# Attention probabilities turned by DMA instead of TensorE, and a band matrix with its columns in another order

## The chip, the cores and the metric

The kernel runs on one core of a Trainium2 chip. A core has TensorE (PE; its weight loads are shown as PEld), VectorE (DVE), ScalarE (ACT), GpSimd (POOL) and SyncE (SP), which here issues every DMA. The metric is the device time of one execution in microseconds (us).

## The reference

Two residual blocks over x of shape 1 x 2048 x 448, in bf16. Block A is a local attention: 16 heads of 28 channels, each position s looks at eight earlier positions s, s-2, ..., s-14. Block B mixes shifted channel groups and then runs a wide feed-forward layer (448 to 1792 to 448).

```
h  = x + A(layernorm(x)),   h2 = h + B(layernorm(h))
A: qkv = x @ wqkv; idx = pos - 2*w for w in 0..7
   logits = einsum("bhsd,bhswd->bhsw", q, k[idx]) * scale   (masked where idx < 0)
   o = einsum("bhsw,bhswd->bhsd", softmax(logits), v[idx]);  return o @ wo
B: h = gelu(layernorm(x) @ w1); hs = shift(h) @ w2; x1 = x + hs
   return x1 + gelu(layernorm(x1) @ w3) @ w4
```

## The kernel before, in words

The 2048 positions are four **blocks** of 512, each block four tiles of 128. Block A runs in phases for each block t: N1 (layer norm), A1 (turn the normalised rows, q and k), V (v), A2 (logits, softmax), A3 (probabilities times v, then wo), B1 (second layer norm, turn, w1, gelu). Block B then runs over five units of 2 or 4 tiles: B2 (w2 and the third layer norm), W3 (w3, gelu) and B3 (w4, store).

The order of the work is written out by hand. Each call of a helper makes one operation with a running number; the list `ORDER` (line 19) is a permutation of these numbers, and `arrange` (line 191) hands every operation to its engine in that order. An engine runs its own operations strictly in that order and waits by semaphore for what an operation needs from others. `OTHER` (line 50) names operations that run on their second engine. Counting the operations in the order in which the code adds them tells what each number in `ORDER` is. In `arrange` a DMA transpose waits for all plain DMAs issued since the transpose before it and for that transpose itself, and a plain DMA waits for the transpose before it. Nearly all instructions are emitted from one line of `emit_engine`, so the profile shows nearly all of them as L983 and they are told apart by tile names: `ps` is PSUM, `bd_r` the band matrix, `pb` the probabilities, `lntm` the normalised rows, `actT` turned activations, `qk_r` the products of queries and keys, and `arena` holds q, k, the turned probabilities `pt`, weights and more.

The parts that the change touches:

- **Turning the normalised rows for q, k and v** (`transposed`, line 568). With "t" TensorE turns a block in 4 steps of 8 transposes (64 partitions each) into two PSUM banks, and two copies bring them to `actT` as 128 x 1024 bf16. With "d" SP issues one DMA transpose. `TURN['A1']` is "ttdd": blocks 0 and 1 by TensorE, 2 and 3 by DMA.
- **Keys shared between groups of 64 positions** (end of `phase_A1`). The key tiles `kr` and `kk` need the last 16 positions of the group before. Four small DMAs a block (`kra`, `krb`, `krc`, `kkp`; the last block has two) copy them from SBUF to SBUF.
- **Turning the probabilities p** (end of `phase_A2`). p lies as 128 rows (head and place) by 8 groups of 80 columns in `pb`. Sixteen matmuls against the identity turn it into two PSUM banks, and two copies of 80 x 512 write `pt` with the row index n outside and the group r inside.
- **The band** (`phase_A3`). For each of four tiles VectorE multiplies `pt`, repeated 8 times, by the 80 x 64 mask `bmask`, repeated 32 times, into an 80 x 2048 bf16 tile of `bd_r` (four buffers). Its columns are ordered (n, g, r), so that the 64 columns of one head n lie side by side. TensorE then runs 32 matmuls a tile: the weights are an 80 x 32 slice of v, the moving operand the 64 columns of one head. Four of them (j = 0 to 3) write to four different groups of 32 PSUM partitions and run at the same time.

Of the kernel before, what the change touches and what calls it, by code (L numbers as in the profile page):

```python
# [6 lines left out]
ALU = mybir.AluOpType  # L7
AX = mybir.AxisListType
BF16 = mybir.dt.bfloat16
# [3 lines left out]
TURN = {'A1': 'ttdd', 'B1': 'dddd', 'B2': 'ddddd'}  # L13
NORM = {'N0': 'vvvv', 'N1': 'avvv', 'B1': 'avvv', 'B2': 'avvvv'}
STATS = {'N1': 'vvva', 'B1': 'avaa', 'B2': 'avvvv'}
NQK, NBD, NLN, NACT, NSM, NO = 3, 4, 2, 4, 1, 6
# [32 lines left out]
"""  # L49
OTHER = """  # L50
102 186 187 381 490 493 496 499 502 505 549
# [229 lines left out]
def bass_sequential_preLN__sliding_local_dilated__mixer_s_mlp__prompt_kernel(  # L281
# [9 lines left out]
    PADK = 16  # L291
# [19 lines left out]
    with ExitStack() as es:  # L311
        def sb(name, shape, dt):
            return es.enter_context(nc.sbuf_tensor(name, shape, dt))
# [6 lines left out]
        bmask = sb("bmask", [KW, 64], BF16)  # L320
        lntm = sb("lntm", [128, NLN, 4, 512], BF16)
# [20 lines left out]
        pb = sb("pb", [128, NSM, NW * KW], BF16)  # L342
# [12 lines left out]
        def arv(off, parts, n):  # L355
            return AR[0:parts, off:off + n]
# [9 lines left out]
        pt = [arv(A_KV + t * KVB + 4 * KVW, KW, 1024) for t in range(NST)]  # L366
# [39 lines left out]
        def dma(chan, out_ap, in_ap, nbytes, eng="sp", **kw):  # L406
            return S.add(eng, "dma_start", chan=chan, nbytes=nbytes, out=out_ap, in_=in_ap, **kw)
# [208 lines left out]
        def setup_late(after):  # L616

            def late(meth, **kw):
                pool(meth, after=after, **kw)

            for lo in (0, 1):
                late("tensor_copy", out=wr_s[:, :, 64 * lo:64 * lo + 64], in_=wqkv_s[:, :, 384 + D * lo:448 + D * lo])
            late("memset", ap=zc[:], constant=0.0)
            for e in range(2):
                late("tensor_copy", out=zc[:, 0:3, e, 16 * e:16 * e + 16], in_=indj[:, 0:3, :])
            late("tensor_copy", out=zc[:, 3, 0, :].rearrange("p (e h) -> p e h", e=2), in_=indj[:, 3:5, :])
            late("memset", ap=onesrow, constant=0.0)
            late("memset", ap=onesrow[0:1, 0:16], constant=1.0)
            late("memset", ap=maskrow, constant=0.0)
            for w in range(1, NW):  # L630
                lo = DIL * (NW - 1 - w)
                late("memset", ap=maskrow[:, 0:64 * w].rearrange("p (r n) -> p r n", n=64)[:, :, lo:lo + DIL], constant=-30000.0)
            late("memset", ap=kk[0][:, :, 0:PADK], constant=0.0)
            late("memset", ap=kr[0][0:64, 0, 0:PADK], constant=0.0)
            late("memset", ap=vw[0:PADK, 0, 0, :], constant=0.0)
            late("memset", ap=gT[:, :, 0:2], constant=0.0)
            late("memset", ap=gT[:, :, 2 + SEQ:4 + SEQ], constant=0.0)
# [30 lines left out]
        def phase_A1(t):  # L668
# [26 lines left out]

            duo(half(X, 0, True), half(Y, 64, False), ((0, 256),))
# [3 lines left out]
            dma("kra%d" % t, kr[t][64:128, :, 0:PADK], kr[t][0:64, :, 64:KW], 64 * 4 * PADK * 2)  # L700
            dma("krb%d" % t, kr[t][0:64, 1:4, 0:PADK], kr[t][64:128, 0:3, 64:KW], 64 * 3 * PADK * 2)
            if t + 1 < NST:
                dma("krc%d" % t, kr[t + 1][0:64, 0, 0:PADK], kr[t][64:128, 3, 64:KW], 64 * PADK * 2)
                dma("kkp%d" % t, kk[t + 1][:, :, 0:PADK], kk[t][:, :, 512:KVW], 128 * 3 * PADK * 2)
# [24 lines left out]
        def phase_A2(t):  # L729
# [34 lines left out]
            mult = dict(out=row(pb, sl * NW * KW + DIL, KW + DIL), in0=row(ls, sl * 512, 64),  # L764
                        in1=bass.AP(zs, sl * 64, [[64 * NSM, 128], [8, NW], [2, 4], [0, NW], [1, DIL]]), op=ALU.mult)
            S.add("dve", "tensor_tensor", alts=[("pool", [("tensor_tensor", mult)])], **mult)
            banks = [_Tile(P_bank), _Tile(P_bank)]

            def turn(h, r):
                part = (TOP, BOT)[h]  # L770
                return (h, dict(out=banks[h](lambda v: v[0:KW, 64 * r:64 * r + 64]), lhsT=pb[part, sl, r * KW:(r + 1) * KW], rhs=ident[part, part],
                                start=True, stop=True), 64)

            steps([turn(h, r) for r in range(NW) for h in range(2)])
            for h, b in enumerate(banks):
                copy(pt[t].rearrange("p (n r) -> p n r", r=NW)[:, 64 * h:64 * h + 64, :], b(lambda v: v[0:KW, :].rearrange("p (r n) -> p n r", r=NW)))

        def phase_A3(t):
            a = _Tile(P_act)
            sl = t % 2  # L780
            for il in range(4):
                bd = _Tile(P_bd)
                b = _Tile(P_bank)
                dve("tensor_tensor", block=True, out=bd(lambda v: v.rearrange("p (n g r) -> p n g r", g=8, r=NW)),
                    in0=pt[t][:, il * 256:il * 256 + 256].rearrange("p (n r) -> p n r", r=NW).unsqueeze(2).broadcast_to([KW, 32, 8, NW]),
                    in1=bmask[:].rearrange("p (g r) -> p g r", r=NW).unsqueeze(1).broadcast_to([KW, 32, 8, NW]), op=ALU.mult)
                mms([(b(lambda v, j=j, lo=128 * c + 64 * a2: v[32 * j:32 * j + 32, lo:lo + 64]),
                      vw[:, sl, 2 * il + a2, (4 * c + j) * 32:(4 * c + j) * 32 + 32],
                      bd(lambda v, lo=(16 * a2 + 4 * c + j) * 64: v[:, lo:lo + 64]), True, True, 64, j)
# [235 lines left out]
```

## Time and profile before

| | |
|---|---|
| median of three runs | 189.47 us (189.41 to 189.87) |
| the profiled execution | 189.32 us |
| its span, first to last instruction | 187.5 us |
| TensorE clock granted | 0.999 |

The profile is of one execution. A busy time is the union of an engine's instructions; idle time is put down to what ended it. The chain of work follows the last instruction back through what released each step. A view by windows gives the busy time of each engine in a stretch.

### The profile page before, as it was taken

Reading aid. Unit: us, or ns where it says so; the run is one execution under the profiler, and the core shown is the slowest. Engines: PE = TensorE matmul, PEld = TensorE weight load, DVE = VectorE, ACT = ScalarE, POOL = GpSimd, SP = SyncE. Lnnn points to the kernel's source line nnn. Section 1 sums busy time; section 2 is a strip of 40 time slices with the busy share of each in tenths; the row PEclk is TensorE's granted clock in tenths of the full one; section 3 lists DMA queues with packets and bytes.
Section 4 is the critical chain, followed back from the end, with each engine's and each line's share of the span. In section 5 each row is a group of like instructions: output and inputs, shape, how many; then the busy total and the mean of one; then the engine's idle time right before and its main releaser. Section 6 shows DMA issues by size and latency. Waiting matters only on the chain.

```text
span 187.5 us, 5641 instructions
## 1 busy us (share of the span) xinstructions
PE 179.2 (96%) x2434; PEld 102.4 (55%) x2434; DVE 126.6 (68%) x224; ACT 123.9 (66%) x282; POOL 29.2 (16%) x63
## 2 busy tenths in 40 slices
PE   6999999999988799999999999999999999999994
PEld 2694434355443345477445555555556665666882
DVE  7799999999999999997297278470057357000503
ACT  4679999989999897988976447505775004822340
POOL 4230000000004101004801200200002662500000
PEclk9999999999999999999999999999999999999999
DMA  5995724676644655453645000371000432400111
GB/s 133 359 286 100 105 59 101 112 177 128 144 129 75 155 144 139 121 154 104 117 126 98 3 0 3 68 149 36 0 0 3 89 96 77 105 3 0 66 36 49
DMA packets 36577, 18.06 MB, mean 96 GB/s; under 512 B 25304, under 2 KB 36040, under 8 KB 36552
## 3 DMA queue, kind: packets, MB, share of 16 engines
q1 hardware_dynamic: 36552, 17.70, 40.2%
q8 instruction: 19, 0.31, 0.7%
q14 instruction: 6, 0.05, 0.1%
HBM read 7.91 MB, written 1.84 MB: 52 GB/s over the span
## 4 chain that ended last, share of the span: by engine, by line
PE 78%; ACT 12%; DVE 4%; DMA 4%; issue 1%; SPq 0%
PE ps L983 78%; ACT arena L983 5%; ACT lntm L983 3%; DMA actT<-lntm 2%; ACT vt L983 2%; DVE st L983 1%; DMA xin<-in_A_x_dram 1%; ACT xin L983 1%; DVE lntm L983 1%; DVE bd_r L983 1%; DVE qk_r L983 1%; ACT rs_x L983 0%; DVE ls L983 0%; DVE mx L983 0%; DVE mv L983 0%
## 5 line engine op out<-in xcount | busy, mean ns | idle before, releaser
L983 PE MATMUL ps<-actT,arena 64*128 64x512 bf16 (+1 forms) x756 | 69.1, 329 | 0.4 <-ACT vt L983 0.4
L983 ACT ACTIVATE h3T<-ps 128x512 bf16<-128x512 f32 (+1 forms) x70 | 31.1, 515 | 40.8 <-PE ps L983 40.5
L983 PEld LDWEIGHTS ps<-actT,arena 64*128 64x128 bf16 x756 | 38.8, 94 | 24.9 <-PE ps L983 0.8
L983 PE MATMUL ps<-arena,h3T 64*128 64x448 bf16 (+2 forms) x434 | 43.7, 343 | 0.1
L983 ACT ACTIVATE arena<-ps 128x512 bf16<-128x512 f32 (+3 forms) x62 | 31.3, 544 | 7.0 <-PE ps L983 6.4
L983 PEld LDWEIGHTS ps<-arena,h3T 64*128 64x128 bf16 (+1 forms) x434 | 26.3, 94 | 16.1 <-PE ps L983 0.5
L983 DVE TENSOR_TENSOR qk_r<-arena 128x4096 bf16<-128x4096 bf16 (+1 forms) x16 | 32.0, 2014 | 0.0
L983 DVE SCALAR_TENSOR_TENSOR qk_r<-ps,mrs,arena 128x448 bf16<-128x448 f32 (+1 forms) x17 | 10.5, 652 | 30.9 <-PE ps L983 25.4
L983 POOL TENSOR_TENSOR arena<-arena,xin 128x448 f32<-128x448 f32 x16 | 16.1, 1037 | 19.8 <-DVE lntm L983 19.8
L983 DVE TENSOR_TENSOR bd_r<-arena,bmask 80x2048 bf16<-80x2048 bf16 x16 | 18.8, 1210 | 0.0
L983 DVE SCALAR_TENSOR_TENSOR arena<-xin,rs_y,ps 128x448 f32<-128x448 bf16 x16 | 10.2, 674 | 11.6 <-PE ps L983 9.6
L983 PE MATMUL ps<-wo_s,actT 64*128 64x448 bf16 x128 | 14.4, 350 | 1.0 <-ACT actT L983 0.7
L983 PE MATMUL ps<-w_s,arena 64*128 64x448 bf16 (+1 forms) x128 | 14.2, 350 | 0.4 <-ACT arena L983 0.3
L983 PE MATMUL ps<-actT,w_s 64*112 64x512 bf16 x112 | 13.4, 379 | 0.8 <-DMA actT<-lntm 0.6
L983 PE MATMUL ps<-arena,actT 64*128 64x448 bf16 x112 | 12.4, 350 | 0.1
L983 ACT ACTIVATE lntm<-xin,nm 128x448 bf16<-128x448 bf16 x16 | 10.5, 663 | 2.4 <-DVE nm L983 2.4
L983 POOL TENSOR_TENSOR pb<-ls,mx 128x512 bf16<-128x512 f32 x2 | 3.5, 1730 | 48.3 <-ACT mx L983 48.3
L983 ACT ACTIVATE actT<-ps 128x512 bf16<-128x512 f32 (+2 forms) x18 | 10.6, 645 | 0.0
L983 PEld LDWEIGHTS ps<-actT,w_s 64*112 64x112 bf16 x112 | 7.1, 127 | 6.3 <-PE ps L983 1.0
L983 PEld LDWEIGHTS ps<-wo_s,actT 64*128 64x128 bf16 x128 | 5.8, 94 | 7.6 <-ACT actT L983 1.9
L983 PEld LDWEIGHTS ps<-w_s,arena 64*128 64x128 bf16 (+1 forms) x128 | 6.4, 94 | 6.6 <-PE ps L983 1.0
L983 DVE BATCH_NORM_STATS2 st<-xin 128x6 f32<-128x448 bf16 x16 | 9.1, 614 | 0.9 <-DMA xin<-in_A_x_dram 0.9
(71 smaller groups left out, 160.9 us busy)
## 6 DMA issues: line engine op xcount, KB each, us to landing
arena<-in_B_w_dram SPq DMA_DIRECT2D x2, 896.0 KB, 5.5
out_dram<-qk_r SPq DMA_DIRECT2D x15, 112.0 KB, 1.8
arena<-in_B_w_dram SPq DMA_DIRECT2D x2, 784.0 KB, 5.0
vw<-vt SPq DMA_DIRECT2D x4, 320.0 KB, 3.2
vw<-vt SPq DMA_DIRECT2D x4, 256.0 KB, 4.7
arena<-in_A_wqkv_dram SPq DMA_DIRECT2D x2, 448.0 KB, 4.5
xin<-in_A_x_dram SPq DMA_DIRECT2D x2, 448.0 KB, 6.9
xin<-in_A_x_dram SPq DMA_DIRECT2D x3, 224.0 KB, 5.2
```

What stands on the lines that cost most here:

```text
L983: inst = getattr(eng, meth)(**kw)
```

## The change

1. `TURN['A1']` becomes "tttt": the normalised rows of blocks 2 and 3 are turned by TensorE.
2. The four key DMAs become copies out of PSUM (helper `last`), on ScalarE, 14 in all.
3. p is turned by one DMA transpose a block; `pb` is padded to 128 columns a group, and `pt` has r outside and n inside. The 16 matmuls and the two copies are gone.
4. The band has its columns ordered (g, r, n). The mask is spread once over an 80 x 2048 tile `band` by GpSimd, so that all three operands of the multiplication have runs of 32 in n. The moving operand of head n is now every 32nd column. `bd_r` has three buffers in place of four.
5. `ORDER` and `OTHER` are new. By the numbers, p of block 2 stays on GpSimd and p of block 3 goes to VectorE; SP issues the turns "B1 of block 0, p of block 2, B1 of block 1" one after another with no plain DMA between them; the second pair of v matmul steps of block 3 moves to just ahead of the w1 matmuls of block 0.

```
-TURN = {'A1': 'ttdd', ...}
+TURN = {'A1': 'tttt', ...}
-NQK, NBD, NLN, NACT, NSM, NO = 3, 4, 2, 4, 1, 6
+NQK, NBD, NLN, NACT, NSM, NO = 3, 3, 2, 4, 1, 6
...
+        band = sb("band", [KW, 2048], BF16)
...
+            late("tensor_copy", out=band[:].rearrange("p (m n) -> p m n", n=32), in_=bmask[:].unsqueeze(2).broadcast_to([KW, 64, 32]))
...
+            def last(b, lo, n):
+                return b(lambda v: v[64:128, 0:256].rearrange("p (j n) -> p j n", j=4)[:, lo:lo + n, 64 - PADK:])
...
-            dma("kra%d" % t, kr[t][64:128, :, 0:PADK], kr[t][0:64, :, 64:KW], 64 * 4 * PADK * 2)
-            dma("krb%d" % t, kr[t][0:64, 1:4, 0:PADK], kr[t][64:128, 0:3, 64:KW], 64 * 3 * PADK * 2)
+            copy(kr[t][64:128, :, 0:PADK], last(X, 0, 4), False)
+            copy(kr[t][0:64, 1:4, 0:PADK], last(Y, 0, 3), False)
             if t + 1 < NST:
-                dma("krc%d" % t, kr[t + 1][0:64, 0, 0:PADK], kr[t][64:128, 3, 64:KW], 64 * PADK * 2)
-                dma("kkp%d" % t, kk[t + 1][:, :, 0:PADK], kk[t][:, :, 512:KVW], 128 * 3 * PADK * 2)
+                copy(kr[t + 1][0:64, 0:1, 0:PADK], last(Y, 3, 1), False)
+                copy(kk[t + 1][:, :, 0:PADK], kk[t][:, :, 512:KVW])
...
-            banks = [_Tile(P_bank), _Tile(P_bank)]
-            def turn(h, r):
...
-            steps([turn(h, r) for r in range(NW) for h in range(2)])
-            for h, b in enumerate(banks):
-                copy(pt[t].rearrange("p (n r) -> p n r", r=NW)[:, 64 * h:64 * h + 64, :], ...)
+            dma_turn("turnp", pt[t].rearrange("p (r n) -> p r n", r=NW), pb[:, sl, :])
...
-                dve("tensor_tensor", block=True, out=bd(lambda v: v.rearrange("p (n g r) -> p n g r", g=8, r=NW)),
-                    in0=pt[t][:, il * 256:il * 256 + 256].rearrange("p (n r) -> p n r", r=NW).unsqueeze(2).broadcast_to([KW, 32, 8, NW]),
-                    in1=bmask[:].rearrange("p (g r) -> p g r", r=NW).unsqueeze(1).broadcast_to([KW, 32, 8, NW]), op=ALU.mult)
+                dve("tensor_tensor", block=True, out=bd(lambda v: v.rearrange("p (g r n) -> p g r n", g=8, r=NW)),
+                    in0=pt[t][0:KW, :].rearrange("p (r n) -> p r n", r=NW)[:, :, 32 * il:32 * il + 32].unsqueeze(1).broadcast_to([KW, 8, NW, 32]),
+                    in1=band[:].rearrange("p (g r n) -> p g r n", g=8, r=NW), op=ALU.mult)
...
-                      bd(lambda v, lo=(16 * a2 + 4 * c + j) * 64: v[:, lo:lo + 64]), True, True, 64, j)
+                      bd(lambda v, n=16 * a2 + 4 * c + j: v[:, n::32]), True, True, 64, j)
```

More of the change, by code (lines that the diff above doesn't have):

```diff
@@ L12 @@
 _LAST = {}
-TURN = {'A1': 'ttdd', 'B1': 'dddd', 'B2': 'ddddd'}
+TURN = {'A1': 'tttt', 'B1': 'dddd', 'B2': 'ddddd'}
 NORM = {'N0': 'vvvv', 'N1': 'avvv', 'B1': 'avvv', 'B2': 'avvvv'}
 STATS = {'N1': 'vvva', 'B1': 'avaa', 'B2': 'avvvv'}
-NQK, NBD, NLN, NACT, NSM, NO = 3, 4, 2, 4, 1, 6
+NQK, NBD, NLN, NACT, NSM, NO = 3, 3, 2, 4, 1, 6
 POWER = {'N1': 'aaaa', 'B1': 'aaaa', 'B2': 'apapp'}
@@ L19 @@
 ORDER = """
[29 rows of a table removed]
[29 rows of a table added]
 """
 OTHER = """
-102 186 187 381 490 493 496 499 502 505 549
+91 103 186 187 383 460 465 499
 """
@@ L341, in bass_sequential_preLN__sliding_local_dilated__mixer_s_mlp__prompt_kernel @@
         indj = ls[:, NSM - 1, 0:40].bitcast(BF16).rearrange("p (c h) -> p c h", c=5)
-        pb = sb("pb", [128, NSM, NW * KW], BF16)
+        pb = sb("pb", [128, NSM, NW * 128], BF16)
         ost = qk_r[:, 0, 0:NO * D].rearrange("p (k n) -> p k n", n=D)
@@ L365, in bass_sequential_preLN__sliding_local_dilated__mixer_s_mlp__prompt_kernel @@
         kr = [arv(A_KV + t * KVB + 3 * KVW, 128, 4 * KW).rearrange("p (j n) -> p j n", j=4) for t in range(NST)]
-        pt = [arv(A_KV + t * KVB + 4 * KVW, KW, 1024) for t in range(NST)]
+        pt = [arv(A_KV + t * KVB + 4 * KVW, 128, 1024) for t in range(NST)]
         maskrow = arv(A_KV + (NST - 1) * KVB, 1, 512)
@@ L763, in phase_A2 @@
             row = lambda v, off, step: bass.AP(v, off, [[v.shape[1] * v.shape[2], 128], [step, NW], [16, 4], [DIL, NW], [1, DIL]])
-            mult = dict(out=row(pb, sl * NW * KW + DIL, KW + DIL), in0=row(ls, sl * 512, 64),
+            mult = dict(out=row(pb, sl * NW * 128 + DIL, 128 + DIL), in0=row(ls, sl * 512, 64),
                         in1=bass.AP(zs, sl * 64, [[64 * NSM, 128], [8, NW], [2, 4], [0, NW], [1, DIL]]), op=ALU.mult)
             S.add("dve", "tensor_tensor", alts=[("pool", [("tensor_tensor", mult)])], **mult)
-            banks = [_Tile(P_bank), _Tile(P_bank)]
-            def turn(h, r):
-                part = (TOP, BOT)[h]
-                return (h, dict(out=banks[h](lambda v: v[0:KW, 64 * r:64 * r + 64]), lhsT=pb[part, sl, r * KW:(r + 1) * KW], rhs=ident[part, part],
-                                start=True, stop=True), 64)
-            steps([turn(h, r) for r in range(NW) for h in range(2)])
-            for h, b in enumerate(banks):
-                copy(pt[t].rearrange("p (n r) -> p n r", r=NW)[:, 64 * h:64 * h + 64, :], b(lambda v: v[0:KW, :].rearrange("p (r n) -> p n r", r=NW)))
+            dma_turn("turnp", pt[t].rearrange("p (r n) -> p r n", r=NW), pb[:, sl, :])
         def phase_A3(t):
```

58 rows, old and new, of the table ORDER are left out of this document.

## The prediction

> **What bounds the kernel now.** I read the busy shares first, then the chain, then the windows on both sides of the first w3 matmul (81.3 us).
>
> ```profile
> PE 179.2 (96%) x2434; PEld 102.4 (55%) x2434; DVE 126.6 (68%) x224; ACT 123.9 (66%) x282; POOL 29.2 (16%) x63
> PE 78%; ACT 12%; DVE 4%; DMA 4%; issue 1%; SPq 0%
> 34.00:81.30 47.30, 43.72 (x824) 21.16 (x823) 46.51 (x62) 43.73 (x99) 3.48 (x4) 1.00 0.56 130
> 81.30:184.30 103.00, 102.94 (x1234) 63.48 (x1231) 47.43 (x104) 52.15 (x114) 20.45 (x23) 1.00 0.25 60
> ```
>
> The reader is to see two kernels in one. From 81.3 us to 184.3 us TensorE never rests (102.94 of 103.00), so a matmul more or less there is time more or less. From 34.0 to 81.3 us three engines are nearly full at once: VectorE 46.51 of 47.30, TensorE 43.72, ScalarE 43.73. All that better scheduling can win in this stretch is the 3.6 us in which TensorE idles. Its largest waits lie around the w1 matmuls of block 0:
>
> ```profile
> 58.57 0.93 PE L983 MATMUL ps<-wo_s,actT 64*128 64x448 bf16 x8 [0.74 <-ACT actT L983]
> 61.47 0.49 PE L983 MATMUL ps<-ident,pb 64*80 64x64 bf16 x16 [0.59 <-POOL arena L983]
> 62.60 3.77 PE L983 MATMUL ps<-actT,w_s 64*112 64x512 bf16 x28 [0.65 <-DMA actT<-lntm]
> 66.30 0.99 PE L983 MATMUL ps<-bd_r,vw 80*32 80x64 bf16 x96
> 67.56 0.93 PE L983 MATMUL ps<-w_s,arena 64*128 64x448 bf16 x8 [0.26 <-ACT arena L983]
> ```
>
> (Start, length, what, and in brackets the idle time before it with its releaser.) The 28 w1 matmuls wait for the DMA transpose of block 0's second layer norm; the only work between was the turn of p.
>
> **The change part by part.** *Turns on TensorE.* The turn of p is 16 matmuls; the turn of a block of normalised rows is 8 + 24 transposes.
>
> ```profile
> 48.06 0.46 PE L983 MATMUL ps<-ident,pb 64*80 64x64 bf16 x16
> 48.36 0.81 PE L983 MATMUL ps<-actT,arena 64*128 64x512 bf16 x6
> 12.73 0.30 PE L983 MATMUL ps<-ident,lntm 64*128 64x64 bf16 x8
> 12.97 0.83 PE L983 MATMUL ps<-actT,arena 64*128 64x256 bf16 x12
> 13.63 0.51 PE L983 MATMUL ps<-ident,lntm 64*128 64x64 bf16 x24
> 13.98 2.81 PE L983 MATMUL ps<-arena,actT 64*128 64x448 bf16 x28
> ```
>
> What counts is start to next start, since the ends overlap: 0.30 us for a p turn, 0.24 + 0.35 = 0.59 us for a block. Four p turns go (-1.2 us), two blocks come (+1.2 us): **zero**.
>
> *The band's moving operand.* This is the step that decides. The 64 columns of a head now lie 64 bytes apart. The volume is 4 blocks x 4 tiles x 8 = 128 groups of four concurrent matmuls.
>
> ```profile
> 100.99 1.29 PE L983 MATMUL ps<-bd_r,vw 80*32 80x64 bf16 x128
> 72.12 1.05 PE L983 MATMUL ps<-qk_r,zc 128*32 128x512 bf16 x16
> L983 PE MATMUL ps<-qk_r,zc 128*32 128x512 bf16 x112 | 7.5, 382 | 0.0
> L983 PE MATMUL ps<-bd_r,vw 80*32 80x64 bf16 x512 | 5.9, 195 | 0.4 <-DVE bd_r L983 0.3
> ```
>
> Now, 128 matmuls (32 groups) last 1.29 us, less the last one's own 0.195: 34 ns a group. The logits matmuls show what a column costs in the same mode: (1.05 - 0.38) / 3 = 0.22 us for 512 columns, 0.44 ns a column, 28 ns for 64. They read runs of 16 adjacent elements; no row shows TensorE reading elements apart. Bounds: **zero** if it reads them as fast, and four streams one after another, 4 x 28 - 34 = 78 ns more a group, **+10.0 us**. Below nothing there is no reason for a gain, the matmuls being the same. Between, the rows of VectorE are the nearest:
>
> ```profile
> L983 DVE TENSOR_TENSOR qk_r<-arena 128x4096 bf16<-128x4096 bf16 x12 | 27.3, 2281 | 0.0
> L983 DVE TENSOR_TENSOR qk_r<-arena 128x2048 bf16<-128x2048 bf16 x4 | 4.9, 1214 | 0.0
> L983 DVE SCALAR_TENSOR_TENSOR qk_r<-ps,mrs,arena 128x448 bf16<-128x448 f32 x15 | 9.6, 679 | 25.0 <-PE ps L983 19.4 <-POOL arena L983 4.9 <-DMA out_dram<-qk_r 0.5
> L983 DVE SCALAR_TENSOR_TENSOR qk_r<-ps,mrs,arena 128x224 bf16<-128x224 f32 x2 | 0.9, 451 | 5.9 <-PE ps L983 5.9
> L983 DVE TENSOR_TENSOR bd_r<-arena,bmask 80x2048 bf16<-80x2048 bf16 x16 | 18.8, 1210 | 0.0
> ```
>
> Adjacent bf16 take VectorE (2281 - 1214) / 2048 = 0.52 ns each, single 4-byte elements (679 - 451) / 224 = 1.02 ns: two neighbours for the price of one access. TensorE's 0.44 ns a column is again about half of such an access. I take it that its rate rests on pairs too, and that elements apart go at half rate: 28 ns more a group, less the 6 ns of slack now in 34, so 2.8 to 3.6 us, and I take **+3.2 us**. The multiplication itself stays at 1210 ns, since it has pairs before and after.
>
> [...]
>
> *ScalarE.* Gone: eight copies of p (seven on ScalarE). Added: four copies of turned rows, 14 small copies.
>
> ```profile
> L983 ACT ACTIVATE arena<-ps 80x512 bf16<-80x512 f32 x7 | 3.9, 591 | 0.0
> L983 ACT ACTIVATE actT<-ps 128x1024 bf16<-128x1024 bf16 x2 | 2.0, 1061 | 0.0
> L983 ACT ACTIVATE mx<-mx 128x64 f32<-128x64 f32 x8 | 2.1, 263 | 0.1
> L983 ACT ACTIVATE rs_y<-rs_x 128x4 f32<-128x4 f32 x12 | 2.5, 208 | 0.2
> L983 ACT ACTIVATE arena<-ps 128x512 bf16<-128x512 f32 x23 | 12.9, 609 | 1.0 <-PE ps L983 0.9
> 8.00:22.00 14.00, 14.00 (x215) 9.75 (x215) 13.44 (x28) 12.09 (x31) 3.20 (x21) 1.00 0.78 176
> 22.00:34.00 12.00, 12.00 (x137) 4.97 (x136) 12.00 (x15) 11.79 (x32) 0.00 (x0) 1.00 0.54 105
> ```
>
> That is 4 x 1.06 - 7 x 0.59 = +0.1 us, and 14 copies of 16 to 64 columns at 0.21 to 0.26 us, +3.3 us. ScalarE is idle 1.9 us from 8 to 22 us, 0.2 us from 22 to 34 us and 3.6 us from 34.0 to 81.3 us: in sum more than it needs, but thin where blocks 1 and 2 are made. I take **0**; if that cover fails, they cost up to their 3.3 us.
>
> *SP and the new transposes.* Fourteen small DMAs leave SP, and the transposes no longer wait for them. The first layer norm's turns of blocks 2 and 3 leave it too, and four half-size transposes come. A half-size one lands after 3.1 us, a full one after 4.5 us:
>
> ```profile
> actT<-lntm SPq DMA_TRANSPOSE x1, 3.1
> actT<-lntm SPq DMA_TRANSPOSE x1, 4.5
> ```
>
> For blocks 0, 1 and 3 much matmul work stands between p and its use, so 3.1 us in place of 0.3 us and two copies is hidden. Block 2 is the tight one. SP issues its turn behind that of B1 of block 0 and must wait until that has landed; behind it wait the turn of B1 of block 1 and, through it, the w1 matmuls of block 1. Call the landing of B1 of block 0 zero. The w1 matmuls of block 0 then run to 3.8. p has landed at 3.1, and VectorE makes one band each 1.2 us: 4.3, 5.5, 6.7, 7.9. TensorE has about 0.3 us (one tile's matmuls) and 0.45 us (half a row of `duo`: eight 64x448 matmuls take 0.93 with their tail) between one band and the next. Its waits: 0.5 before the first, 0.45 before the second, none before the third, 0.9 before the fourth, **1.9 us**. Now the bands are made during the w1 matmuls (three stand ready at 66.3). Against this the v steps of block 3 moved ahead of the w1 matmuls (14 matmuls, half of the 2.81 us row) fill **1.4 us** of today's 0.59 + 0.65 us and of the gap around the p turn. Net **+0.5 us**. In those waits the slower band matmuls of three tiles are hidden, **-0.6 us**.
>
> *Small parts.* GpSimd spreads the mask once, early, on an engine at 16%: bounded by 0 and its own length, some 2 us (its 128x512 multiplication took 2.38 us). I take 0, because the first band is needed long after. Three band buffers for four: 0, as VectorE, not the buffers, sets the pace.
>
> ```profile
> 59.03 2.38 POOL L983 TENSOR_TENSOR pb<-ls,mx 128x512 bf16<-128x512 f32 x1 [47.70 <-ACT mx L983]
> ```
>
> **Sum**, on the profiled execution's 189.32 us (187.5 us of span and 1.8 us around it): 0 (turns) + 3.2 (band) + 0 (ScalarE) + 0.5 (waits) - 0.6 (hidden) = 192.4 us. The median of the runs shown lies 0.15 us higher, so **192.6 us**.
>
> **The rivals**, each from the median. (1) *TensorE reads every 32nd column at full rate* and the new order removes waits: the 0.74, 0.59 and 0.65 us go and 0.7 us of the new ones stay. 189.5 - 2.0 + 0.7 = **188.2 us**, faster. It decides if a group stays below 36 ns. For it: ScalarE copied p (80x512) out of PSUM at a stride of 256 bytes in 591 ns, no slower than the contiguous 128x512 copies (609 ns). [...] (2) *Full rate, but ScalarE becomes the bound*: of 3.3 us of small copies a third shows, 189.5 + 1.1 = **190.6 us**. The chain, 12% on ScalarE, speaks for it. (3) *The four streams get in each other's way*, one after another: +10.0 us, less 1.9 us that the waits hide: **197.6 us**. The equal rate of 0.44 ns for four at once speaks against a narrow port for neighbours, but says nothing for elements apart.
>
> **How the numbers follow.** Forecast 0.49 (190.3 to 194.5 us), rival 1 0.26, rival 2 0.10, rival 3 0.15. A difference of about 0.3%, 0.57 us, is what a measurement here can tell from none. Faster: nearly all of rival 1 and little else, 0.26. Within: 0.07. Slower: the rest, 0.67. The range, 187.3 to 198.0 us, runs from rival 1 with more waits gone to rival 3; the forecast's own is 190.3 to 194.5 us.
>
> **What would show it.** First the span of one tile's 32 band matmuls, today:
>
> ```profile
> 69.39 0.42 PE L983 MATMUL ps<-bd_r,vw 80*32 80x64 bf16 x32
> ```
>
> It would be about 0.65 us at half rate and 1.0 in rival 3. Then block 3's band matmuls, which stand where TensorE has no idle time to take them: they alone should cost 0.8 us. Then waits of the band matmuls on `bd_r` in block 2, between the w1 matmuls of blocks 0 and 1. The forecast fails if 128 band matmuls in one piece still take 1.3 us, or if waits on ScalarE appear in place of that.

## The result, and the profile after

The changed kernel takes 198.33 us (198.09 to 198.78) beside 189.73 us for the kernel before: a ratio of 1.046, with a 95% interval from 1.0434 to 1.0485. The profiled execution spans 197.1 us, 9.6 us more than before. The forecast of 192.6 us had the sign and the place right, but the change is 8.6 us where 3.1 were foretold: the time lies above the forecast's own range (up to 194.5 us) and just above the whole one (up to 198.0 us).

Busy shares, chain and windows of the changed kernel (the windows are cut where its first w3 matmul starts, at 87.76 us):

```profile
PE 189.2 (96%) x2434; PEld 104.9 (53%) x2434; DVE 126.9 (64%) x223; ACT 124.0 (63%) x292; POOL 31.1 (16%) x63
PE 82%; ACT 11%; DVE 3%; DMA 1%; issue 1%; SPq 0%
34.00:87.76 53.76, 52.53 (x837) 27.80 (x834) 46.32 (x65) 46.71 (x109) 4.28 (x4) 1.00 0.46 102
87.76:193.80 106.04, 105.97 (x1219) 60.46 (x1220) 48.23 (x103) 50.26 (x115) 19.58 (x21) 1.00 0.25 57
```

TensorE executes as many matmuls as before (2434), but is busy 10.0 us longer; VectorE and ScalarE are not. The stretch from 34 us to the first w3 matmul grew from 47.3 to 53.8 us, though TensorE's idle time in it fell from 3.6 to 1.2 us. The stretch behind it, where TensorE never rests, grew by 3.0 us.

The groups by line name what grew. The first row is the band's matmuls (195 ns each and 5.9 us before), then two groups that stayed as they were, and the band's multiplication:

```profile
L979 PE MATMUL ps<-bd_r,vw 80*32 80x64 bf16 x512 | 17.3, 295 | 0.9 <-DVE bd_r L979 0.9
L979 PE MATMUL ps<-wo_s,actT 64*128 64x448 bf16 x128 | 14.3, 350 | 0.1
L979 PE MATMUL ps<-arena,actT 64*128 64x448 bf16 x112 | 12.5, 350 | 0.1
L979 DVE TENSOR_TENSOR bd_r<-arena,band 80x2048 bf16<-80x2048 bf16 x16 | 18.9, 1214 | 7.9 <-DMA arena<-pb 7.4
```

The same 512 matmuls are busy 11.4 us longer, and each lasts 100 ns longer. In the timeline one tile's 32 matmuls take 1.11 us, where they took 0.42:

```profile
38.79 1.11 PE L979 MATMUL ps<-bd_r,vw 80*32 80x64 bf16 x32
39.83 1.47 PE L979 MATMUL ps<-actT,arena 64*128 64x512 bf16 x16
41.23 1.13 PE L979 MATMUL ps<-bd_r,vw 80*32 80x64 bf16 x32
42.30 0.82 PE L979 MATMUL ps<-actT,arena 64*128 64x512 bf16 x6
```

0.69 us for each of 16 tiles is 11.0 us. The time grew by less (8.6 us), since 2.4 us of it went into TensorE's idle time.

### The profile page after: what moved, and what is told of

The parts are those of the page before. It is cut to its first block, busy times and chain, and to the rows that moved or that the text cites. A ratio compares the mean times of both kernels' runs of the same rounds, so it can differ in the third digit from the quotient of the medians.

```text
span 197.1 us, 5614 instructions
## 1 busy us (share of the span) xinstructions
PE 189.2 (96%) x2434; PEld 104.9 (53%) x2434; DVE 126.9 (64%) x223; ACT 124.0 (63%) x292; POOL 31.1 (16%) x63
## 4 chain that ended last, share of the span: by engine, by line
PE 82%; ACT 11%; DVE 3%; DMA 1%; issue 1%; SPq 0%
PE ps L979 82%; ACT arena L979 4%; ACT actT L979 3%; ACT lntm L979 2%; ACT vt L979 2%; DMA xin<-in_A_x_dram 1%; DVE lntm L979 1%; DVE st L979 1%; DVE bd_r L979 1%; DVE qk_r L979 1%; ACT xin L979 0%; SPq L979 0%; ACT rs_x L979 0%; ACT rs_y L979 0%; ACT ls L979 0%
## 5 line engine op out<-in xcount | busy, mean ns | idle before, releaser
L979 PEld LDWEIGHTS ps<-actT,arena 64*128 64x128 bf16 x756 | 36.7, 94 | 30.3 <-ACT actT L979 1.9
L979 PE MATMUL ps<-arena,h3T 64*128 64x448 bf16 (+2 forms) x434 | 45.0, 343 | 0.0
L979 PEld LDWEIGHTS ps<-arena,h3T 64*128 64x128 bf16 (+1 forms) x434 | 23.8, 94 | 18.1 <-issue 0.6
L979 ACT ACTIVATE arena<-ps 128x512 bf16<-128x512 f32 (+5 forms) x64 | 28.1, 482 | 5.2 <-PE ps L979 4.7
L979 POOL TENSOR_TENSOR arena<-arena,xin 128x448 f32<-128x448 f32 x16 | 18.9, 1196 | 48.7 <-DVE lntm L979 28.0
L979 ACT ACTIVATE actT<-ps 128x512 bf16<-128x512 f32 (+2 forms) x24 | 16.4, 706 | 13.7 <-PE ps L979 13.7
L979 DVE TENSOR_TENSOR bd_r<-arena,band 80x2048 bf16<-80x2048 bf16 x16 | 18.9, 1214 | 7.9 <-DMA arena<-pb 7.4
L979 PE MATMUL ps<-bd_r,vw 80*32 80x64 bf16 x512 | 17.3, 295 | 0.9 <-DVE bd_r L979 0.9
L979 PEld LDWEIGHTS ps<-bd_r,vw 80*32 80x32 bf16 x512 | 13.7, 112 | 5.1 <-DVE bd_r L979 1.8
L979 DVE TENSOR_SCALAR lntm<-arena,mv,rs_y 128x512 bf16<-128x512 f32 x14 | 7.5, 593 | 4.8 <-ACT rs_y L979 2.8
```

The lines of the kernel that those rows point to most:

```text
L979: inst = getattr(eng, meth)(**kw)
```

## The experiments

**Theory:** the 64-byte step of the band's moving operand costs 0.69 us a tile, and all other parts of the change come to about nothing. **Rival:** the new order, the copies on ScalarE and the DMA turns cost the time, and the slow matmuls are hidden in waits. A second question was what the step costs and why: the prediction had guessed pairs; pieces of 16 bytes (the lines of the expectations, which no run before e3 to e5 shows), a bank hit again and again, and four streams in each other's way were the others.

### Each half alone: e1, e11 and e2

e1 undoes the read only. e11 is the same kernel again beside other runs.

```
-  bd(lambda v, n=16 * a2 + 4 * c + j: v[:, n::32])
+  bd(lambda v, lo=(16 * a2 + 4 * c + j) * 64: v[:, lo:lo + 64])
```

> The changed kernel, but the band matmuls read 64 adjacent columns again (the wrong ones for the head, so the attention output is not the reference's); everything else of the change stays. Theory (the strided read costs 0.69 us a tile, 11 us in all, and the rest of the change gives some back): a tile's 32 matmuls fall from 1.11 to 0.42 us and the time to about 187.5 us (186 to 189.5), below the kernel before. Rival (the new order, the copies on ScalarE and the DMA turns cost the time, the read is hidden in waits): it stays at 194 us or more.

> The run with adjacent columns once more, beside these two on one chip, since its interval was wide (1.003 to 1.011): again 1.005 to 1.008 of the kernel before, which is what all other parts of the change cost together.

e2 does the opposite edit to the kernel before.

> The kernel before, in which only the band matmuls read every 32nd column (the wrong ones, so the attention output is not the reference's). Theory: 0.42 to 1.1 us a tile, and +9 to +11 us, 198.5 to 200.5 us. Rival: under +4 us.

Measured: e1 has a ratio of 1.0068 to the kernel before (1.0026 to 1.0111), e11 1.0064 (1.0016 to 1.0113), e2 1.0434 (1.038 to 1.0488; 198.02 us, a little below the 198.5 us expected). So the read alone makes the kernel before as slow as the whole change, and without it the change costs 0.65%, about 1.2 us. e1 was expected *below* the kernel before; that part of the theory failed: the rest of the change gives nothing back. Where the 0.65% lies can't be read: the two executions that were profiled (189.87 and 190.00 us) are the fastest of their runs and no slower than the kernel before. The timelines, e1 first, then e2:

```profile
38.29 0.43 PE L979 MATMUL ps<-bd_r,vw 80*32 80x64 bf16 x32
40.12 0.42 PE L979 MATMUL ps<-bd_r,vw 80*32 80x64 bf16 x32
```

```profile
41.87 1.11 PE L983 MATMUL ps<-bd_r,vw 80*32 80x64 bf16 x32
43.88 2.02 PE L983 MATMUL ps<-bd_r,vw 80*32 80x64 bf16 x64
107.32 3.91 PE L983 MATMUL ps<-bd_r,vw 80*32 80x64 bf16 x128
```

The matmuls' length follows the step in both orders. The rival is refuted.

### How far apart: e3, e4 and e5

The column order is free as long as multiplication and matmul agree. With runs of K neighbours the matmul reads every K-th column, and VectorE writes runs of K. (Shortened: the two inputs of the multiplication are read in the same order.)

```
-  out=bd(lambda v: v.rearrange("p (g r n) -> p g r n", g=8, r=NW))
+  out=bd(lambda v: v.rearrange("p (q g r e) -> p g r q e", g=8, r=NW, e=K))
-  bd(lambda v, n=16 * a2 + 4 * c + j: v[:, n::32])
+  bd(lambda v, n=16 * a2 + 4 * c + j: v[:, n // K * 64 * K + n % K : n // K * 64 * K + 64 * K : K])
...
```

> The changed kernel with the band's columns ordered (n/2, g, r, n%2): the matmuls read every 2nd column (4 bytes apart), the multiplication writes runs of 2. If the price hangs on elements per 16-byte line, 4 in a line keep full rate: 0.42 us a tile and about 187.5 us. If it hangs on adjacent pairs, a tile takes 0.65 us or more and the time is 190.5 us or more. If VectorE loses its pairwise rate at runs of 2, a band takes 2.3 us in place of 1.21.

> The changed kernel with the columns ordered (n/8, g, r, n%8): the matmuls read every 8th column (16 bytes apart). Theory of one element per 16-byte line: as slow as every 32nd column, 1.1 us a tile, 197.5 to 199 us. Rival, that the 64-byte step hits one bank again and again: clearly faster than that, 0.7 us a tile or less.

> The changed kernel with the columns ordered (n/4, g, r, n%4): the matmuls read every 4th column, 8 bytes apart, two elements in each 16-byte line; the multiplication writes runs of 4. If two elements of a line keep the full rate (the theory of lines): 0.42 us a tile. If VectorE also keeps 1.21 us a band: about the time with adjacent columns, 189 to 191 us. Rival: two in a line are not enough, 0.65 us a tile or more, 192 us or more. If VectorE slows as with runs of 2 (1.95 us) but less, a band of 1.4 to 1.6 us and 192 to 195 us.

The groups by line of e3 (K = 2, 4 bytes apart), e5 (K = 4, 8 bytes) and e4 (K = 8, 16 bytes), each with one tile's matmuls from the timeline:

```profile
L979 DVE TENSOR_TENSOR bd_r<-arena,band 80x2048 bf16<-80x2048 bf16 x16 | 30.0, 1952 | 7.4 <-DMA arena<-pb 7.4
L979 PE MATMUL ps<-bd_r,vw 80*32 80x64 bf16 x512 | 6.9, 200 | 7.3 <-DVE bd_r L979 4.6 <-DVE ls L979 1.6 <-DVE nmr L979 0.9
38.81 0.43 PE L979 MATMUL ps<-bd_r,vw 80*32 80x64 bf16 x32
```

```profile
L979 DVE TENSOR_TENSOR bd_r<-arena,band 80x2048 bf16<-80x2048 bf16 x16 | 18.9, 1216 | 7.5 <-DMA arena<-pb 7.4
L979 PE MATMUL ps<-bd_r,vw 80*32 80x64 bf16 x512 | 10.2, 238 | 1.7 <-DVE bd_r L979 0.9 <-issue 0.7
38.77 0.66 PE L979 MATMUL ps<-bd_r,vw 80*32 80x64 bf16 x32
```

```profile
L979 DVE TENSOR_TENSOR bd_r<-arena,band 80x2048 bf16<-80x2048 bf16 x16 | 18.9, 1214 | 7.9 <-DMA arena<-pb 7.4 <-PE ps L979 0.5
L979 PE MATMUL ps<-bd_r,vw 80*32 80x64 bf16 x512 | 17.6, 294 | 0.9 <-DVE bd_r L979 0.9
70.15 1.11 PE L979 MATMUL ps<-bd_r,vw 80*32 80x64 bf16 x32 [0.86 <-DVE bd_r L979]
```

A group of four is 4/31 of the tile's span less the last matmul's own length:

| columns apart | elements in 16 bytes | one tile | a group of four | a column |
|---|---|---|---|---|
| 2 bytes (e1) | 8 | 0.42 us | 29 ns | 0.45 ns |
| 4 bytes (e3) | 4 | 0.43 us | 30 ns | 0.46 ns |
| 8 bytes (e5) | 2 | 0.66 us | 54 ns | 0.85 ns |
| 16 bytes (e4) | 1 | 1.11 us | 105 ns | 1.6 ns |
| 64 bytes (the change) | 1 | 1.11 us | 105 ns | 1.6 ns |

Neighbouring pairs don't matter (4 bytes apart takes 0.43 us a tile, adjacent 0.42), nor does a bank that a 64-byte step would hit (16 bytes apart takes the same 1.11 us). What fits, as an estimate from the table, is one 16-byte piece in 1.6 to 1.8 ns for a stream, however much of it is used: 4 x 0.46, 2 x 0.85 and 1 x 1.6 ns. (The first of these is only a bound, since adjacent columns are no faster.) That it is the piece of 16 bytes was read from these distances, not shown apart from them. Of the expectations, e5's rival holds (0.65 us a tile or more, 192 us or more), and so does the theory of lines in e4 and, for TensorE, in e3.

As whole kernels: e5 192.71 us, ratio 1.0124 (1.0085 to 1.0163), the fastest form of the changed kernel that computes the reference; e4 198.32 us, as slow as the change; e3 198.22 us, for another reason: VectorE takes 1.95 us for a band written in runs of 2, and TensorE then waits 7.3 us for it and for what stands behind it on VectorE. Runs of 4 keep VectorE at 1.216 us and cost TensorE about half its rate (54 ns a group in place of 29). None of the run lengths tried gives both.

### Four streams or each by itself: e6 and e7

```
-  for c in range(4) for a2 in range(2) for j in range(4)])
+  for j in range(4) for c in range(4) for a2 in range(2)])
```

> The changed kernel, the 32 band matmuls of a tile in the order j outermost, so that eight in a row write to the same 32 PSUM partitions and the four streams can't run at the same time. If the four streams share one read rate for elements apart (0.51 ns an element), nothing is lost by taking them in turn: 1.0 to 1.2 us a tile, about 198 us. If each stream by itself goes four times slower (2 ns an element), a tile takes 4 us and the time is 240 us or more.

> As the run with the streams in turn, but reading adjacent columns (the wrong ones for the head, so the output is not the reference's). It is what one stream after another costs without the stride: 32 x 28 ns = 0.9 us and the last one's tail, 1.0 to 1.1 us a tile, 197 to 199 us. If it equals the strided run in turn, the stride costs a single stream nothing.

The timeline and the tile's own view (shortest, median, longest in ns) of e6, 64 bytes apart, then of e7, adjacent:

```profile
38.33 2.33 PE L979 MATMUL ps<-bd_r,vw 80*32 80x64 bf16 x32
L979 PE MATMUL ps<-bd_r,vw x512: 267/287/296, 38.3 to 148.1; 80*32 80x64 bf16 x171
```

```profile
40.84 0.80 PE L979 MATMUL ps<-bd_r,vw 80*32 80x64 bf16 x32
L979 PE MATMUL ps<-bd_r,vw x512: 190/193/203, 40.8 to 122.9; 80*32 80x64 bf16 x171
```

Taken in turn, a matmul starts every 66 ns with the step and every 20 ns without it. These are means, and the single starts in the trace tell more. In the first tile of e6 the first four matmuls start one by one, 96 to 110 ns apart; the next 24 start two by two, the second of a pair 6 to 16 ns behind the first, a pair every 97 to 111 ns; the last four again start one by one, 110 ns apart. So a tile is some 20 turns of about 110 ns. In e7's first tile the first and last four start 28 to 34 ns apart, and those between overlap two by two as in e6. The first five matmuls of the tile by themselves, e6 and then e7, show the single stream: the last one's own length taken off, (0.71 - 0.29) / 4 = 0.11 us from start to start with the step, (0.31 - 0.19) / 4 = 0.03 us without.

```profile
38.33 0.71 PE L979 MATMUL ps<-bd_r,vw 80*32 80x64 bf16 x5
40.84 0.31 PE L979 MATMUL ps<-bd_r,vw 80*32 80x64 bf16 x5
```

So a stream with no neighbour takes 110 ns for 64 columns with the step, and four at once take 105 ns: **each stream is slower by itself**, and its neighbours add nothing that shows. If four streams shared one rate, in turn would have cost nothing more than at once (1.1 us); it costs 2.33 us. The expected 4 us is not reached, since for most of a tile two streams run side by side after all. That the two are neighbouring groups of PSUM partitions is inferred, as the trace does not name a matmul's group: every eighth matmul, where a new group would begin, is a little shorter in e6 (268 to 273 ns in place of 287) and stands second in the first of four pairs.

Is it TensorE's clock that sets the 110 ns? The whole times of e6 (221.88 us) and e7 (196.61 us, just below the 197 to 199 expected) are of one execution each, and e6 holds stretches in which the granted clock is half. One of them answers the question. First comes the window of the band matmuls (stretch, length, busy time and number, then the granted clock, 0.50, and two figures for DMA), then two groups of matmuls in it. The last row has the band matmuls of adjacent columns in a stretch of e9 (a run of the next section) that also has a granted clock of 0.50, from 42.7 to 49.3 us:

```profile
84.30:97.80 13.50, 5.94 (x94) 0.50 0.32 84
L979 PE MATMUL ps<-bd_r,vw 80*32 80x64 bf16 x94 | 6.2, 286 | 0.0
L979 PE MATMUL ps<-wo_s,actT 64*128 64x448 bf16 x24 | 5.0, 570 | 0.0
```

```profile
L986 PE MATMUL ps<-bd_r,vw 80*32 80x64 bf16 x64 | 1.3, 242 | 0.0
```

At half the clock the matmuls of wo take 570 ns in place of 350, and band matmuls of adjacent columns 242 in place of 193. With the step they take 286 ns, as at full clock. So the price of the step does not follow TensorE's granted clock. Where it is paid no trace shows.

### The keys: e8, e9 and e10

e8 is the kernel before with the key copies of the change.

> The kernel before with the shared keys copied out of PSUM by ScalarE in place of the 14 small DMAs, each copy right behind the key eviction of its bank, the order otherwise that of before. By the prediction's step (ScalarE 0, nothing else gained): 189.5 to 190.5 us. Rival (ScalarE is the bound from 22 to 34 us and the 14 copies show): 191 us or more.

Measured: 191.31 us, ratio 1.0067 (1.004 to 1.0094). The rival holds: the 14 copies in place of the 14 DMAs cost 1.3 us. Where it shows in the timeline of e8: the matmuls that wait for the v copy of ScalarE start at 36.36 us (35.51 before), the w1 matmuls at 64.58 us (62.60 before).

```profile
36.36 1.04 PE L993 MATMUL ps<-actT,arena 64*128 64x512 bf16 x8 [0.38 <-ACT vt L993]
64.58 3.77 PE L993 MATMUL ps<-actT,w_s 64*112 64x512 bf16 x28 [0.96 <-DMA actT<-lntm]
```

e9 and e10 give the changed order the DMAs again, with adjacent columns and with runs of 4.

```
-  copy(kr[t][64:128, :, 0:PADK], last(X, 0, 4), False)
+  dma("kra%d" % t, kr[t][64:128, :, 0:PADK], kr[t][0:64, :, 64:KW], 64 * 4 * PADK * 2)
...
```

> The changed kernel with both costs that the runs found undone: the matmuls read adjacent columns (the wrong ones for the head, so the output is not the reference's) and the shared keys go by the 14 small DMAs again, each right behind the key evictions that it needs. What is left of the change is the turn of p by DMA, the turns of blocks 2 and 3 on TensorE and the new order. If the copies on ScalarE cost here what they cost in the kernel before (0.7%), it is 0.7% below the run with adjacent columns beside it, and equal to the kernel before (189 to 190.5 us). Rival: the DMAs now stand in the way of the turns of p, and it is as slow or slower.

> The changed kernel with columns 8 bytes apart (runs of 4) and the keys by DMA. By the costs found so far: 1.012 - 0.007 = 1.005 of the kernel before, 190.5 to 191.5 us. Rival as above: 1.012 or more.

Both came out far slower, as their rivals said: e9 1.0638 (1.0574 to 1.0702), e10 1.0649 (1.0545 to 1.0752). VectorE's timeline in e9 shows the products of queries and keys waiting for the key DMAs, TensorE's waits (us in all, times, longest) show who pays:

```profile
24.81 1.22 DVE L986 TENSOR_TENSOR qk_r<-arena 128x2048 bf16<-128x2048 bf16 x1 [2.49 <-DMA arena<-arena]
42.56 1.23 DVE L986 TENSOR_TENSOR qk_r<-arena 128x2048 bf16<-128x2048 bf16 x1 [3.36 <-DMA arena<-arena]
58.19 1.22 DVE L986 TENSOR_TENSOR qk_r<-arena 128x2048 bf16<-128x2048 bf16 x1 [2.19 <-DMA arena<-arena]
```

```profile
PE ps L986 <- DVE qk_r L986: 3.7, 1, 3.7
PE ps L986 <- DVE bd_r L986: 3.2, 2, 2.1
PE ps L986 <- DVE nm L986: 2.3, 1, 2.3
PE ps L986 <- DMA actT<-lntm: 1.7, 1, 1.7
```

The new order makes the last key group just ahead of its use. There the DMAs come 2.2 to 3.4 us too late, while in the order of before VectorE waits for none of them, and the copy only loads a full engine (ScalarE is busy 11.78 of the 12.00 us from 22 to 34 us in e8). The waits are not all of it: the granted clock is 0.50 for 10.2 us of e9 (from 42.6 to 49.4 and from 63.1 to 66.5 us). Of the 12.7 us between the profiled executions of e9 and e1, 8.0 us are idle time of TensorE and 4.7 us are longer matmuls. What brought the clock down is not shown. So the price of the copies in the new order could not be read by taking them back alone; that they make up e1's 0.65% is a likeness of two numbers, not shown.

## Why the prediction was wrong, point by point

**The band's moving operand: the step that failed, in its size.** The mechanism was forecast: TensorE goes slower on columns apart (105 ns a group at 64 bytes, 29 ns for neighbours). The price was set at half rate, +3.2 us, from VectorE's pairs of bf16 (0.52 ns an element beside 1.02 ns for a single one of 4 bytes); that TensorE keeps such pairs was the author's estimate, and columns 4 bytes apart at 30 ns a group refute it. Measured are 105 ns a group, 0.69 us a tile and +11.0 us in all, more than three times as much. (The 34 ns a group that the prediction started from hold the gaps between four tiles; one tile's own 0.42 us give 29 ns.) Half rate is what 8 bytes apart gives: e5's 0.66 us a tile is the 0.65 us of the forecast. The +11.0 us lie above the upper bound of +10.0 us, though a group stays below the bound's 112 ns: a matmul is also 0.10 us longer in itself (295 ns beside 195), which shows at the end of each of 16 tiles (1.6 us), and the prediction has no term for that. The bound came near by luck, as it assumed that no stream is slowed by itself, only by its neighbours; e6 shows the reverse (110 ns for one stream, 105 for four). What was missing was the count of elements in 16 bytes: VectorE's rows hold only neighbours or 4-byte elements, and say nothing of elements further apart. Two elements in 16 bytes are not enough for TensorE here: four keep the full rate (30 ns a group, e3), two give about half of it (54 ns, e5), one a little over a quarter (105 ns, e4).

**Rival 3** came near the time, 197.6 us, by luck: its mechanism is what e6 refutes (110 ns for a stream by itself).

**What the waits hide:** forecast 0.6 us for the smaller price; 2.4 us of TensorE's idle time was filled by the larger one. The 0.8 us foretold for block 3, where nothing can hide, is 2.8 us (4 x 0.69), near the 3.0 us by which that stretch grew.

**ScalarE: 0 taken, up to 3.3 us if the cover fails.** e8 shows 1.3 us in the order of before. The cover was thin where the prediction said so, and it was still priced at nothing. The copies' own times were about right (175 to 280 ns, 2.9 us in all, 3.3 foretold):

```profile
L979 ACT ACTIVATE arena<-ps 64x64 bf16<-64x64 f32 x4 | 0.8, 210 | 0.0
L979 ACT ACTIVATE arena<-arena 128x48 bf16<-128x48 bf16 x3 | 0.8, 280 | 0.0
L979 ACT ACTIVATE arena<-ps 64x48 bf16<-64x48 f32 x4 | 0.8, 204 | 0.1
L979 ACT ACTIVATE arena<-ps 64x16 bf16<-64x16 f32 x3 | 0.5, 175 | 0.0
```

**Block 2's waits: +1.9 us of new ones, 1.4 us of old ones filled.** TensorE around the w1 matmuls of block 0, and SP's waits, in the changed kernel:

```profile
65.11 1.73 PE L979 MATMUL ps<-arena,actT 64*128 64x448 bf16 x14
66.68 3.19 PE L979 MATMUL ps<-actT,w_s 64*112 64x512 bf16 x28
70.73 1.11 PE L979 MATMUL ps<-bd_r,vw 80*32 80x64 bf16 x32 [0.86 <-DVE bd_r L979]
```

```profile
SPq L977 <- POOL pb L979: 3.3, 1, 3.3
```

The v steps do fill the wait: the w1 matmuls no longer wait for their turn. The first band is waited for, 0.86 us (0.5 foretold); the other waits are covered by the slow matmuls themselves. Where the matmuls are fast, as the 1.9 us assumed, e1 waits 1.1 us for bands and e11 1.3 us. But the reason given for the late turn of p was not the whole one: SP's wait of 3.3 us ended with GpSimd's p, not with the landing of the turn ahead.

**Turns on TensorE: zero.** A block's 32 transposes take 0.53 us from start to next start (25.61 to 26.14), against 0.59 us foretold.

```profile
25.61 0.69 PE L979 MATMUL ps<-ident,lntm 64*128 64x64 bf16 x32
26.14 0.73 PE L979 MATMUL ps<-arena,actT 64*128 64x448 bf16 x6
```

**The multiplication** stays at 1214 ns, **the mask's spreading** on GpSimd costs nothing that shows, and the DMA turns of p land after 3.1 us, all as foretold. With three band buffers VectorE waits once, 0.5 us, for the slow band matmuls. Not priced was the start: the first q and k matmuls begin at 8.72 us after a wait of 0.96 us for the copies of turned rows (7.95 us before), but at 8.14 us in e1 with the same order.

No version here beats the kernel before: without the step the change still costs 0.65%, and of the column orders tried those that VectorE writes at full rate (1214 to 1216 ns a band) put a head's columns at least 8 bytes apart. The kernel before has both, adjacent columns and 1210 ns a band, because its `pt` has r inside; whether VectorE could write that order at full rate from a `pt` that a DMA turned, with n inside, was not tried.

## What to carry to other kernels

Before a layout is changed to suit the engine that writes it, count how many elements of the moving operand lie in each 16 bytes that TensorE will read: four keep the full rate here (30 ns a group of 64-column matmuls, where adjacent columns take 29), two about halve it (54 ns), one leaves little over a quarter (105 ns). A cost with no row in the trace must be bounded by what one stream can lose by itself as well as by what it loses to its neighbours. And a cover of 0.2 us in 12 us is no cover: price the work beneath it.

## What the runs showed of the hardware that was not expected

- A 64-column matmul four at a time takes 29 and 30 ns a group with columns 2 and 4 bytes apart (e1, e3), 54 ns at 8 bytes (e5) and 105 ns at 16 or 64 bytes (e4, the change); its own length grows from 195 ns (2 bytes) to 238 ns (8 bytes) and 295 ns (64 bytes).
- VectorE multiplies 2048 bf16 in 1.216 us when it writes runs of 4 and in 1.95 us when it writes runs of 2 that lie 256 bytes apart, with the same number of elements and all inputs in order.
- One stream alone takes as long as four at once: 110 and 105 ns for 64 columns 64 bytes apart, about 29 ns in both cases for adjacent ones.
- At half the granted clock a 448-column matmul grows from 350 to 570 ns and a 64-column one of adjacent columns from 193 to 242 ns, but one with columns 64 bytes apart stays at 286 ns.
